# A kernel of attention and two matrix chains on one core: its first loads in three parts, its first scores in two steps, its last store in two halves, and some loads at other places in the plan

## Chip, core and metric

The kernel runs on one core of a Trainium2 chip. The metric is the device time of one execution in microseconds (us), the median of several runs. The engines are named as in the profile: PE is TensorE (PEld its weight loads), ACT is ScalarE, DVE is VectorE, POOL is GpSimd, SP is SyncE, which here only issues transfers (DMAs).

## The reference, cut to what matters

```python
# 4 batches, 8 heads, 512 local and 32 global positions, head size 64
s_g = scale * q_g @ k_all.T ;  out_g = softmax(s_g) @ v_all      # the 32 global queries see all keys
s_l = [scale * q_l @ k_g.T, banded(scale * q_l @ k_l.T, |i - j| <= 32)]
out_l = softmax(s_l) @ [v_g, v_l]                                 # local queries: global keys and a band
x = concat(out_g, out_l)  ->  (2176 tokens, 512)
h = x @ w_in                  # 512 -> 2048
g = h * clip(h + 3, 0, 6) / 6
y = g @ w_out                 # 2048 -> 512
z = max(y @ w1, y @ w2, y @ w3)   # 512 -> 768
out = z @ w_out2              # 768 -> 512
```

Inputs and output are float32; the weights come as 64-bit words that the kernel decodes (three vector steps and a copy for each block).

## The kernel before

The work has four stages that overlap at their borders. **Attention** goes over 4 batches times 4 pairs of heads (`pair`): load Q, K and V of the pair (tiles `qr`, `kr`, `vr`), scores into PSUM banks `s` or `bank` (L449), the row maximum with the band mask on DVE (L463), the exponential on ACT (L469), a sum and its reciprocal, the scaling on POOL (L494, tile `tbuf`), the transposes on PE (L506), their copies to `pt` (L410), and the product with V into `o` (L532). Each pair has two groups u = 0 and 1 of two query tiles v = 0 and 1 of 128 rows, so a group's scores are eight matmuls. After each two pairs the 32 global queries of both are done (`globals_`: L566, L592, L607). **First** (L673, three-pass products of split float32 operands) makes `x @ w_in` as soon as weights are decoded (`decode`, loads `raw<-in_w_in` at L642) and rows of x are there; it is put between the steps of the attention on PE. The gated result goes to DRAM (`gsA`, `gsB`, `gsC`). **Second** (L837) reads it back for `w_out`, **third** (L961, `quad`) makes the three products with w1, w2 and w3 and their maximum, written to DRAM as `hd`, and **fourth** (`single` L1116, `double` through `quad`) reads `hd` back (the loads of h, L1102 and L1128) and makes the output, which `send` stores (L1089).

No engine's order is written out by hand. Every step is an `op` with an engine, an assumed duration, a due time and the buffers that it reads and writes; `Plan.order` walks through time, and among the steps that could start on a free engine takes the one with the lowest due time. The sequence that results is the program; on each engine it runs in exactly this order. A changed duration, due time or split of one step can therefore change what stands where on every engine much later. `LAG` sets how early the loads of the third stage's weights may start.

At the very start PE writes ones into the score banks (`fill`, L395, four matmuls of 128 columns for each of six banks), and the first scores wait for all of them (`after=full`). The first pair's Q is loaded in two parts on SP's queue and its K in two parts on ACT's queue; part 0 holds what group u = 0 needs:

```python
for n, (t, src, cut, size) in enumerate(((Q, q_n, 256, NQ + SG), (K, k_n, 352, NK))):
    for i, (a, z) in enumerate(((0, cut), (cut, size)) if b + pr == 0 else ((0, size),)):
        e, issue = ("ACT", nc.scalar) if b + pr == 0 and n else ("SP", nc.sync)
```

The last `double` leaves two tiles of 128 tokens; the second is stored in two column halves of 128 x 256 (128 KB each), the last of them after the last copy out of PSUM on ACT (L412).

## Time and profile before

| | us |
|---|---|
| median of 3 runs | 733.19 |
| the 3 runs | 730.5, 733.19, 733.71 |
| the profiled execution, as timed | 731.45 |
| its span, first to last instruction | 729.2 |
| PE busy in it | 717.7 |
| DVE, ACT, POOL busy | 535.3, 411.0, 189.8 |
| PE's last matmul ends, from the span's start | 726.2 |

The time of an execution is its span and 2.25 us around it. Busy time is the time in which an engine had at least one instruction under way; since matmuls follow each other in a pipeline, a busy PE can still have been kept waiting for some hundred nanoseconds between two of them.

### The profile page before, as it was taken

How to read it: one execution, taken by the hardware profiler on the slowest of the kernel's cores; microseconds unless marked ns; L12 is line 12 of the kernel's file. 1: busy time of each engine (PE TensorE's matmuls, PEld its weight loads, DVE VectorE, ACT ScalarE, POOL GpSimd, SP SyncE). 2: the span in 40 equal slices, each digit the busy share in tenths (PEclk: the TensorE clock that was granted, in tenths of full speed). 3: DMA queues.
4: the chain of work that ended last, by engine and by line, in shares of the span. 5: the costliest groups of instructions: out<-in, count | busy, mean ns of one | idle time of the engine just before them, and what ended most of it. 6: DMA issues, size and time to landing. Idle time of an engine off the chain costs nothing.

```text
span 729.2 us, 14100 instructions
## 1 busy us (share of the span) xinstructions
PE 717.7 (98%) x5329; PEld 638.1 (88%) x5329; DVE 535.3 (73%) x1100; ACT 411.0 (56%) x858; POOL 189.8 (26%) x225
## 2 busy tenths in 40 slices
PE   8999999999999999999999999999999999999998
PEld 6777878788888899988898899898999999998998
DVE  6979676546777766589976768999877886485881
ACT  7997889555544444356663457673644334253552
POOL 6685869322203122111000001121210220011210
PEclk9999999999999999999999999999999999999999
DMA  7455775424368884676565669401453562355652
GB/s 279 129 180 193 253 256 192 153 72 165 140 209 295 317 307 171 233 260 195 174 206 156 202 196 312 127 2 32 133 172 134 173 228 69 102 170 198 175 159 88
DMA packets 73140, 131.34 MB, mean 180 GB/s; under 512 B 4976, under 2 KB 43632, under 8 KB 72048
## 3 DMA queue, kind: packets, MB, share of 16 engines
q1 hardware_dynamic: 72784, 130.13, 53.6%
q8 instruction: 42, 0.69, 0.4%
q10 hardware_dynamic: 288, 0.31, 0.1%
q14 instruction: 26, 0.21, 0.1%
HBM read 84.93 MB, written 45.48 MB: 179 GB/s over the span
## 4 chain that ended last, share of the span: by engine, by line
PE 79%; DMA 6%; DVE 5%; ACT 4%; POOL 3%; issue 2%; SPq 0%; ACTq 0%; DVEq 0%; POOLq 0%
PE bank L961 31%; PE bank L673 21%; PE bank L837 20%; PE s L506 2%; ACT tbuf L469 2%; POOL rq L655 2%; PE o L532 2%; PE s L449 1%; DMA raw<-in_w_in_dram 1%; DMA gsA<-rq 1%; DMA kr<-in_kn_dram 1%; PE bank L1116 1%; POOL tbuf L494 1%; DVE rr L655 1%; PE s L607 1%
## 5 line engine op out<-in xcount | busy, mean ns | idle before, releaser
L673 PE MATMUL bank<-rx,rw 128*128 128x512 f32 (+1 forms) x960 | 199.1, 363 | 1.1 <-DVE rq L685 1.1
L673 PEld LDWEIGHTS bank<-rx,rw 128*128 128x128 f32 x960 | 161.2, 188 | 26.8 <-issue 4.3
L837 PE MATMUL bank<-rr,rw 128*128 128x320 f32 (+2 forms) x912 | 155.1, 331 | 1.0 <-DVE rr L655 0.9
L837 PEld LDWEIGHTS bank<-rr,rw 128*128 128x128 f32 x912 | 140.2, 188 | 15.0 <-DVE rr L655 1.9
L961 PE MATMUL bank<-rw,rr 128*128 128x256 f32 (+2 forms) x648 | 99.7, 302 | 1.1 <-DVE rf L973 0.7
L961 PEld LDWEIGHTS bank<-rw,rr 128*128 128x128 f32 x648 | 90.6, 188 | 6.1 <-DVE rf L973 1.1
L760 ACT CAST rr<-fw 128x1024 fp32r<-128x1024 f32 (+2 forms) x76 | 62.1, 820 | 52.3 <-PE bank L837 40.5
L655 DVE TENSOR_TENSOR rr<-fw,rr 128x1024 fp32r<-128x1024 f32 (+2 forms) x76 | 71.7, 947 | 25.1 <-ACT rr L760 24.4
L655 POOL TENSOR_TENSOR rf<-rf 128x256 f32<-128x256 f32 (+2 forms) x35 | 37.5, 1080 | 157.2 <-DVE rf L655 58.8
L469 ACT ACTIVATE tbuf<-tbuf,nm 128x224 f32<-128x224 f32 x128 | 60.6, 479 | 11.0 <-DVE nm L463 10.9
L685 DVE SCALAR_TENSOR_TENSOR rq<-rq,bank 128x512 f32<-128x512 f32 (+1 forms) x60 | 37.1, 619 | 38.4 <-ACT rq L683 38.1
L494 POOL TENSOR_TENSOR tbuf<-tbuf,nm 128x448 f32<-128x448 f32 x64 | 61.0, 973 | 8.4 <-DVE nm L485 4.9
L683 ACT ACTIVATE rq<-bank,three 128x512 f32<-128x512 f32 (+1 forms) x60 | 37.9, 632 | 43.5 <-PE bank L673 40.3
L410 ACT COPY rf<-bank 128x512 f32<-128x512 f32 (+2 forms) x72 | 33.2, 468 | 39.9 <-PE bank L961 29.5
L961 PE MATMUL bank<-rw,re 128*128 128x256 f32 (+2 forms) x369 | 54.2, 292 | 0.7 <-DVE bank L410 0.7
L961 PE MATMUL bank<-re,rr 128*128 128x512 f32 x222 | 54.8, 391 | 0.0
L655 POOL TENSOR_TENSOR rq<-rq 128x256 f32<-128x256 f32 (+2 forms) x45 | 38.5, 861 | 54.1 <-DVE rq L655 49.5
L961 PEld LDWEIGHTS bank<-rw,re 128*128 128x128 f32 x369 | 49.4, 188 | 2.4 <-DVE bank L410 0.9
L961 PEld LDWEIGHTS bank<-re,rr 128*128 128x128 f32 x222 | 40.8, 188 | 8.1
L1055 DVE TENSOR_TENSOR rf<-rf,bank 128x320 f32<-128x320 f32 (+2 forms) x72 | 37.0, 528 | 13.0 <-PE bank L961 11.7
L463 DVE CUSTOM_DVE_ANT_0 tbuf<-s,mask 128x224 f32<-128x224 f32 x112 | 36.9, 383 | 6.7 <-PE s L449 6.4
L506 PE MATMUL s<-ident,tbuf 128*128 128x128 f32 x256 | 33.9, 276 | 0.4 <-POOL tbuf L494 0.2
(131 smaller groups left out, 1047.4 us busy)
## 6 DMA issues: line engine op xcount, KB each, us to landing
fw<-gsB SPq DMA_DIRECT2D x28, 512.0 KB, 4.8
raw<-in_w_dram SPq DMA_DIRECT2D x24, 512.0 KB, 4.3
fw<-gsC SPq DMA_DIRECT2D x28, 320.0 KB, 3.6
raw<-in_w_in_dram SPq DMA_DIRECT2D x16, 512.0 KB, 4.0
raw<-in_w_o_dram SPq DMA_DIRECT2D x16, 512.0 KB, 4.9
fw<-gsA SPq DMA_DIRECT2D x28, 256.0 KB, 2.8
gsB<-rq SPq DMA_DIRECT2D x6, 1024.0 KB, 5.1
rf<-hd SPq DMA_DIRECT2D x14, 384.0 KB, 4.9
```

The lines of the kernel that those rows point to most:

```text
L463: nc.vector.tensor_tensor_reduce(out=tb[hh]()[:, v, 0:WIN], in0=sb[hh]()[:, v * WIN:v * WIN + WIN], in1=mask[i // 2]()[:, i % 2], scale=-0 ...
L469: nc.scalar.activation(out=t, in_=t, func=ACTF.Exp, scale=-1.0, bias=nm()[:, 0, hh, v:v + 1], accum_out=nm()[:, 1, hh, v:v + 1])
L494: nc.gpsimd.tensor_tensor(out=t, in0=t, in1=r, op=ALU.mult)
L506: nc.tensor.transpose(FB[u][hh]()[:, at:at + 128], TB[u][hh]()[:, v, kb * 128:kb * 128 + 128], ident)
L655: ENG[e].tensor_tensor(out=out, in0=a, in1=b, op=f)
L673: nc.tensor.matmul(ps()[:, 0:m], lhsT=w[:, i, k], rhs=xs(c)[:, j, k], start=(k == 0 and s == 0), stop=(k == KC - 1 and s == 2))
L683: op("ACT", us, lambda ps=ps, m=m, out=out: nc.scalar.activation(out=out(), in_=ps()[:, 0:m], func=ACTF.Relu, bias=three), -100, r=[ps], w ...
L685: op("DVE", us, lambda ps=ps, m=m, out=out: nc.vector.scalar_tensor_tensor(out=out(), in0=out(), scalar=6.0, in1=ps()[:, 0:m], op0=ALU.min ...
L760: op("ACT", act(n) + 0.01, lambda: nc.scalar.copy(out=out(0), in_=src()), due, r=r, w=[(w, "hi")], what=what + "_hi")
L837: nc.tensor.matmul(A[e]()[:, 0:n], lhsT=w[:, 2 * fp + f, u, e], rhs=r[:, v, f], start=(seed is None and fp + f + s == 0), stop=(fp == 3 an ...
L961: nc.tensor.matmul(bank()[:, 0:n], lhsT=w[:, u, k], rhs=r[:, v, k], start=(start and k + s == 0), stop=(k == K - 1 and s == 2), skip_group ...
L1055: op("DVE", dve(n), lambda q=q, src=src, mv=mv: nc.vector.tensor_tensor(out=mv(q)(), in0=mv(q)(), in1=src(), op=ALU.max), -200, r=[bank], ...
```

## The change

It makes these edits. The first pair's Q is cut at columns 128 and 256 and its K at 224 and 352, so that part 0 is what query tile v = 0 needs (Q 128 x 128 and K 128 x 224), part 1 what v = 1 needs beyond it, and part 2 the rest. The first group's scores become two steps, one for each v, each with its own parts of Q and K as inputs, and what they write is named by v, so that the row maxima of v = 0 can follow the first step. `fill` writes 448 columns of each bank (three times 128 and once 64) and not 512. The last store goes out in two halves of 64 partitions, one issued by SP and one by ACT. The loads of h in `double` are due 18 and not 12 us before their product, and `LAG` is 94 and not 92.

```diff
-LAG = 92.0
+LAG = 94.0
...
     def fill(bank):
-        for j in range(4):
-            nc.tensor.matmul(bank[:, 128 * j:128 * j + 128], lhsT=ones, rhs=ones, start=True, stop=True)
+        for a in range(0, 2 * WIN, 128):
+            n = min(128, 2 * WIN - a)
+            nc.tensor.matmul(bank[:, a:a + n], lhsT=ones, rhs=ones[:, 0:n], start=True, stop=True)
...
-        for n, (t, src, cut, size) in enumerate(((Q, q_n, 256, NQ + SG), (K, k_n, 352, NK))):
-            for i, (a, z) in enumerate(((0, cut), (cut, size)) if b + pr == 0 else ((0, size),)):
+        for n, (t, src, cuts, size) in enumerate(((Q, q_n, (128, 256), NQ + SG), (K, k_n, (WIN, 352), NK))):
+            for i, (a, z) in enumerate(zip((0, *cuts), (*cuts, size)) if b + pr == 0 else ((0, size),)):
...
-                    out=t()[:, a:z], in_=src[b, pr][:, a:z]), s0 - 6 + i, w=[(t, i)] if b + pr == 0 else [t],
+                    out=t()[:, a:z], in_=src[b, pr][:, a:z]), s0 - 6 + i / 2, w=[(t, i)] if b + pr == 0 else [t],
...
-            need = [(Q, grp[0]), *((K, u) for u in range(grp[0] + 1))] if len(grp) == 1 else [Q, K]
-            head = op("PE", 0.62 * k, scores, s1, r=need, after=full if b + pr == 0 else (),
-               w=[x for u in grp for x in SB[u]] + [(t, "held") for u in grp for t in TB[u]], what="scores")
+            if b + pr + grp[0] == 0:
+
+                for v in range(2):
+                    head = op("PE", 0.31, lambda v=v, scores=scores: scores((v,)), s1 + v / 2, r=[(Q, v), *((K, x) for x in range(v + 1))],
+                              w=[(x, v) for x in SB[0]] + [(t, "held") for t in TB[0]], after=full, what="scores")
+            else:
+                need = [(Q, 2), (K, 1), (K, 2)] if b + pr == 0 else [Q, K]
+                head = op("PE", 0.62 * k, scores, s1, r=need,
+                          w=[x for u in grp for x in SB[u]] + [(t, "held") for u in grp for t in TB[u]], what="scores")
...
-    def send(o, t0, due, a=0, k=2):
-
-        def store():
+    def send(o, t0, due, a=0, k=2, parts=0):
+
+        def store(h=None):
             b, p = divmod(t0, SL)
             col = slice(256 * a, 256 * (a + k))
-            if b < B:
+            if h is not None:
+                (nc.scalar if h else nc.sync).dma_start(out=out[b * NQ + SG + p + 64 * h:b * NQ + SG + p + 64 * h + 64, col],
+                                                        in_=o()[64 * h:64 * h + 64, col])
+            elif b < B:
...
-        op("SP", 0.7, store, due, r=[(o, j) for j in range(a, a + k)], kb=128 * k, what="store")
+        r = [(o, j) for j in range(a, a + k)]
+        if parts:
+            for h in range(2):
+                op(("SP", "ACT")[h], 0.7, lambda h=h: store(h), due, r=r, kb=64 * k, what="store")
+        else:
+            op("SP", 0.7, store, due, r=r, kb=128 * k, what="store")
...
-               t - 12, r=rows(ts[i]), w=[(W, 1 - i)], kb=384, what="hload")
+               t - 18, r=rows(ts[i]), w=[(W, 1 - i)], kb=384, what="hload")
...
-            send(O[i], ts[i], t + 8 + i + (k - 1) / 4, a, k)
+            send(O[i], ts[i], t + 8 + i + (k - 1) / 4, a, k, last and i + a == 1)
```

Where it moves instructions: on PE the first difference is in the fills, the eight first scores stand in the same order with one wait more among them, and from the third pair on the attention's steps and `first` are interleaved otherwise. Counted over PE's whole order, its matmuls stand in 151 runs of one source line before and in 138 after; up to the end of the attention these are 139 and 128, and visits to `first` among them 42 and 35. No matmul is added or taken away: 28 fills, seven of them shortened, and 4,597 others. On DVE, ACT and POOL the order differs from the first batch on through the third stage; PE's last 868 matmuls and DVE's last 113 instructions, in the third and fourth stage, stand as before.

The first place is the start. On PE, the first scores before, with the semaphores that they wait for (`DMAHW0` to `DMAHW7` are those of the transfers, `kr` and `qr` the tiles of K and Q):

```order
L449 MATMUL s_162<-kr,qr 64x128 [waits DMAHW1_49,DMAHW0_49]
L449 MATMUL s_163<-kr,qr 64x128
L449 MATMUL s_162<-kr,qr 64x192
L449 MATMUL s_163<-kr,qr 64x192
L449 MATMUL s_162<-kr,qr 64x192
L449 MATMUL s_163<-kr,qr 64x192
L449 MATMUL s_162<-kr,qr 64x160
L449 MATMUL s_163<-kr,qr 64x160
```

And on PE at the same place after the change:

```order
L450 MATMUL s_162<-kr,qr 64x128 [waits DMAHW1_49,DMAHW0_49]
L450 MATMUL s_163<-kr,qr 64x128
L450 MATMUL s_162<-kr,qr 64x192
L450 MATMUL s_163<-kr,qr 64x192
L450 MATMUL s_162<-kr,qr 64x192 [waits DMAHW3_49,DMAHW2_49]
L450 MATMUL s_163<-kr,qr 64x192
L450 MATMUL s_162<-kr,qr 64x160
L450 MATMUL s_163<-kr,qr 64x160
```

The second four now wait for parts of their own, and the first four for smaller ones. On SP's queue at the start, before (V is `vr`, the second pair's loads are whole tiles of 576 and 608 columns):

```order
L426 DMA qr<-in_qn_dram 128x256
L426 DMA qr<-in_qn_dram 128x320
L426 DMA qr<-in_qn_dram 128x576
L426 DMA kr<-in_kn_dram 128x608
L429 DMA vr<-in_v_dram 128x640 x2
L426 DMA qr<-in_qn_dram 128x576 [waits DMAHW0_49]
L426 DMA kr<-in_kn_dram 128x608 [waits DMAHW1_49]
L642 DMA raw<-in_w_in_dram 128x4x256 [waits DMAHW2_49]
```

And after, where there is one transfer more ahead of the second pair's, and the loads of V wait for the first parts to land, because the eight semaphores are all taken:

```order
L427 DMA qr<-in_qn_dram 128x128 x2
L427 DMA qr<-in_qn_dram 128x320
L427 DMA qr<-in_qn_dram 128x576
L427 DMA kr<-in_kn_dram 128x608
L430 DMA vr<-in_v_dram 128x640 [waits DMAHW0_49]
L430 DMA vr<-in_v_dram 128x640 [waits DMAHW1_49]
L427 DMA qr<-in_qn_dram 128x576 [waits DMAHW2_49]
L427 DMA kr<-in_kn_dram 128x608 [waits DMAHW3_49]
```

The order on ACT's queue is K in three parts and not two, then its first exponentials. The second place is the attention's middle, on PE around the transposes of the third set of global queries (`tg`; `rx,rw` are operands of `first`), before:

```order
L673 MATMUL bank_135<-rx,rw 128x512 x3
L673 MATMUL bank_134<-rx,rw 128x512 x3
L506 MATMUL s_162<-ident,tbuf_142 128x128 x4
L506 MATMUL s_163<-ident,tbuf_144 128x128 x4
L673 MATMUL bank_134<-rx,rw 128x512 x3
L506 MATMUL s_164<-ident,tbuf_146 128x128 x4
L506 MATMUL s_165<-ident,tbuf_148 128x128 x4
L592 MATMUL s_166<-ident,tg 128x128 x4
L592 MATMUL s_162<-ident,tg 128x128
L673 MATMUL bank_134<-rx,rw 128x512 x3
L566 MATMUL s_163<-kr,qr 64x288 x2
L566 MATMUL s_164<-kr,qr 64x256 x2
```

And after:

```order
L680 MATMUL bank_134<-rx,rw 128x512 x3
L680 MATMUL bank_135<-rx,rw 128x512 x12
L680 MATMUL bank_134<-rx,rw 128x512 x3
L513 MATMUL s_163<-ident,tbuf_142 128x128 x4
L513 MATMUL s_164<-ident,tbuf_144 128x128 x4
L680 MATMUL bank_134<-rx,rw 128x512 x6
L513 MATMUL s_165<-ident,tbuf_146 128x128 x4
L513 MATMUL s_166<-ident,tbuf_148 128x128 x4
L599 MATMUL s_162<-ident,tg 128x128 x4
L599 MATMUL s_163<-ident,tg 128x128
L680 MATMUL bank_134<-rx,rw 128x512 x3
```

The same steps stand there with more of `first` between them at a visit. On SP's queue in the first batch, the loads of the weights of `first` (`raw`) among those of a pair, before:

```order
L699 DMA gsA<-rq 128x768
L642 DMA raw<-in_w_in_dram 128x4x256
L426 DMA qr<-in_qn_dram 128x576
L429 DMA vr<-in_v_dram 128x640
L426 DMA kr<-in_kn_dram 128x608
L429 DMA vr<-in_v_dram 128x640
L699 DMA gsA<-rq 128x1024
```

And after, where K is no longer behind a V, and the block of weights stands behind Q, K and V:

```order
L706 DMA gsA<-rq 128x768
L427 DMA qr<-in_qn_dram 128x576
L427 DMA kr<-in_kn_dram 128x608
L430 DMA vr<-in_v_dram 128x640
L649 DMA raw<-in_w_in_dram 128x4x256
L430 DMA vr<-in_v_dram 128x640
L706 DMA gsA<-rq 128x768
```

The third place is the end. On SP the rows from the first load of h on are the same as before but for the last, a store of 128x256 that becomes one of 64x256; the loads of h (L1128, now L1143) stand where they stood. On ACT the last rows before are these:

```order
L412 ACTIVATE rf<-bank_2649 128x256 [waits DMAHW3_49,DMAHW1_49,PE_49]
L412 ACTIVATE rf<-bank_2651 128x256 [waits DMAHW0_49,PE_49]
L1201 UNCONDITIONAL_BRANCH
```

And after, with the store's second half behind the last copy:

```order
L413 ACTIVATE rf<-bank_2624 128x256 [waits DMAHW5_49,DMAHW3_49,PE_49]
L413 ACTIVATE rf<-bank_2626 128x256 [waits DMAHW2_49,PE_49]
L1096 DMA out_dram<-rf 64x256 [waits Activation_49]
L1216 UNCONDITIONAL_BRANCH
```

## Rows read from the trace of the kernel before

**Rows 1.** The page: span, and each engine's busy time.
```profile
span 729.2 us, 14100 instructions
PE 717.7 (98%) x5329; PEld 638.1 (88%) x5329; DVE 535.3 (73%) x1100; ACT 411.0 (56%) x858; POOL 189.8 (26%) x225
```

**Rows 2.** Busy time by stretch: from:to, length, then each engine's.
```profile
0.00:3.90 3.90, 2.74 (x24) 2.48 (x24) 1.02 (x15) 1.28 (x1) 3.34 (x15) 1.00 0.51 149
3.90:28.10 24.20, 22.38 (x317) 16.61 (x319) 20.77 (x96) 21.67 (x81) 15.03 (x24) 1.00 0.67 236
28.10:205.00 176.90, 174.27 (x1778) 141.30 (x1773) 117.82 (x372) 132.71 (x370) 96.05 (x121) 1.00 0.51 177
205.00:600.00 395.00, 392.83 (x2357) 360.08 (x2356) 314.61 (x491) 199.07 (x317) 59.49 (x54) 1.00 0.58 191
600.00:726.20 126.20, 125.47 (x863) 117.67 (x862) 81.12 (x129) 55.90 (x91) 15.92 (x13) 1.00 0.44 141
```

**Rows 3.** The timeline at the start: start, length, engine and line.
```profile
0.73 0.90 ACTq L426 DMA_DIRECT2D kr<-in_kn_dram  x2
...
2.60 0.91 SPq L429 DMA_DIRECT2D vr<-in_v_dram  x2
2.73 1.06 PE L395 MATMUL bank<-ones 128*128 128x128 bf16 x8
...
5.52 0.39 DVE L463 CUSTOM_DVE_ANT_0 tbuf<-s,mask 128x224 f32<-128x224 f32 x1 [3.67 <-PE s L449]
```

**Rows 4.** Transfers issued in the first 12 us: count, size, time to landing.
```profile
kr<-in_kn_dram ACTq DMA_DIRECT2D x1, 176.0 KB, 3.1
qr<-in_qn_dram SPq DMA_DIRECT2D x1, 128.0 KB, 2.9
kr<-in_kn_dram ACTq DMA_DIRECT2D x1, 128.0 KB, 3.5
```

**Rows 5.** The chain that ended last, its pieces in the first 30 us.
```profile
3.91 1.50 PE s L449 x16
...
5.95 4.29 ACT tbuf L469 x18
...
22.58 0.29 DVE rx L549
...
27.56 1.83 PE o L532 x32
```

**Rows 6.** PE's timeline in the attention: visits to `first` and what follows.
```profile
31.10 0.97 PE L673 MATMUL bank<-rx,rw 128*128 128x512 f32 x3
32.00 1.00 PE L532 MATMUL o<-pt,vr 128*64 128x128 f32 x16
...
107.59 7.10 PE L673 MATMUL bank<-rx,rw 128*128 128x512 f32 x30
114.53 1.03 PE L506 MATMUL s<-ident,tbuf 128*128 128x128 f32 x8
115.32 0.95 PE L673 MATMUL bank<-rx,rw 128*128 128x512 f32 x3
116.11 1.03 PE L506 MATMUL s<-ident,tbuf 128*128 128x128 f32 x8
```

**Rows 7.** PE's waits between 28.1 and 726.2 us: total, times, longest.
```profile
PE bank L673 <- DVE rq L685: 1.1, 1, 1.1
PE s L449 <- DMA kr<-in_kn_dram: 1.1, 2, 0.6
```

**Rows 8.** The timeline at the end: the last copy, and SP's last stores.
```profile
718.12 8.85 SPq L1089 DMA_DIRECT2D out_dram<-rf  x5
...
726.22 0.38 ACT L412 ACTIVATE rf<-bank 128x256 f32<-128x256 f32 x1 [2.81 <-PE bank L961]
```

**Rows 9.** The stores issued from 724 us on, with time to landing.
```profile
out_dram<-rf SPq DMA_DIRECT2D x2, 128.0 KB, 1.7
out_dram<-rf SPq DMA_DIRECT2D x1, 256.0 KB, 2.0
```

More of the change, by code (lines that the diff above doesn't have):

```diff
@@ L393, in fill @@
     def fill(bank):
-        for j in range(4):
-            nc.tensor.matmul(bank[:, 128 * j:128 * j + 128], lhsT=ones, rhs=ones, start=True, stop=True)
+        for a in range(0, 2 * WIN, 128):
+            n = min(128, 2 * WIN - a)
+            nc.tensor.matmul(bank[:, a:a + n], lhsT=ones, rhs=ones[:, 0:n], start=True, stop=True)
     def filled(bank, after=()):
-        return op("PE", 0.43, lambda: fill(bank), -100, after=after, rel=0.4, what="fill")
+        return op("PE", 0.38, lambda: fill(bank), -100, after=after, rel=0.4, what="fill")
     full = [filled(bank) for bank in (*sbanks[:4], banks[6], banks[7])]
@@ L438, in pair, with scores @@
                 NM[u] = Buf(T["nm"])
-            def scores(grp=grp, SB=SB):
+            def scores(vs=(0, 1), grp=grp, SB=SB):
                 for u in grp:
-                    for v in range(2):
+                    for v in vs:
                         i = 2 * u + v
```

## The prediction

> **What bounds the kernel now.** I read the page's busy times first: PE is busy 717.7 of 729.2 us, and no other engine is near it [rows 1]. So the end comes where PE's own list of work ends, and the question for each edit is whether PE starts earlier, waits less or has less to do. The busy time by stretch says where PE is not busy [rows 2]. Up to 3.9 us it does only the fills. From 3.9 to 28.1 us, the first batch, it is idle 24.20 - 22.38 = 1.82 us while ACT is busy 21.67 us of 24.20. From 28.1 to 726.2 us it is idle in 698.1 us for 2.63 + 2.17 + 0.73 = 5.53 us, in waits of half a microsecond to one. After 726.2 us it has nothing left. All idle time between its first score and its last matmul is thus 7.35 us: what waiting alone can give back.
>
> The chain of waits tells which work sets the pace at the start: K's landing, the scores, then exponential after exponential on ACT from 5.95 us on, a DVE stretch from 22.58 us, and from 27.56 us PE [rows 5]. The reader is to see there that until about 27 us PE waits for the softmax, and from then on the softmax is fed into a PE that always has some of `first` to do.
>
> **The change part by part.**
>
> *First loads and scores.* The first scores begin at 3.91 us [rows 5], 0.08 after K's first part landed (issued 0.73, landing 3.1 later [rows 3, 4]). Of two parts issued at 0.73 the one of 176 KB took 3.1 and the one of 128 KB 2.9 us: 48 KB for 0.2 us. The new first part of K has 112 KB, 64 less, so it lands some 0.27 sooner, at 3.56, and Q's first part of 64 KB sooner than that. This is an estimate from two rows on two queues; its bounds are no gain at all and, if landing went by size alone, a part that is there before PE is free. Scores then begin at about 3.64.
>
> The fills must be over by then. The last eight begin at 2.73 and end 1.06 us later, one each 0.107 us if the last is as long as their 0.31 [rows 3], so the last starts at 3.48 and PE could issue a score at 3.58, shortened or not. Six shorter fills ahead of it give between 0 and 0.32 us, which nothing needs: I cost them at zero. If their cover goes, because K lands faster than I think, at most 0.3 us shows.
>
> The second gain is larger. The row maximum waits for all sixteen score records, 1.50 us [rows 5], and begins at 5.52 [rows 3]. Now it waits for half of them: 3.64 + 0.75 + 0.10 (as now from 5.42 to 5.52) = 4.49. That is 1.03 us earlier, and with it ACT's first exponential, at 5.95 now [rows 5]. The second step needs K's second part, which is issued one ACT issue later (0.90/2 = 0.45 us [rows 3]) and completes the 176 KB that landed at 3.83 before; I put it at 4.3, under the first step. The third parts go out 0.45 us later on both queues; the one of K took 3.5 us from 1.18 [rows 4], so 5.1 at the latest against scores that need it after the second step and a fill, not before 5.5. The loads of V now stand behind a wait for the first parts: from 2.60 us [rows 3] to about 3.6, ten microseconds ahead of the first product with V on PE, which is behind the transposes. Behind them in SP's queue the third pair's loads and the first weight block shift by tenths; I cost that at nothing while ACT has the sixteen exponentials of two pairs to do.
>
> What does PE get of the 1.03 us? About the 0.27 by which its own scores move, at least. At most all, if it loses 0.76 of its 1.82 us idle. I take 0.8, near the upper end, since ACT is the busy engine of the stretch and PE's idle time there is what ACT leaves. Bounds: 0.2 to 1.0.
>
> *The new order in the attention.* PE's list has 11 runs of one kind of matmul fewer up to the end of the attention. What a run costs is seen at `first`: thirty matmuls in one visit take 114.53 - 107.59 = 6.94 us, 0.231 each, while three alone hold PE for 32.00 - 31.10 = 0.90 us, not 0.69 [rows 6]. Thirteen such short visits between 31 and 116 us, of which this is the longest and the last, 116.11 - 115.32, the shortest, hold it 0.79 to 0.90 us: 0.10 to 0.21 more than three in a long run, 0.15 in the middle. Eleven runs fewer are 11 x 0.15 = 1.65 us. Lower bound nothing, if these changes of kind hid waits that now show as idle; upper bound 11 x 0.21 = 2.3. I take 1.65, because from 28.1 us on only 2.63 us of 176.9 are idle, so PE was working, not waiting, at most of these places.
>
> *The waits after 28.1 us.* A new order keeps none of them in its place. Two are for K (1.1 us) and one for the gated result (1.1 us) [rows 7]. I leave the sum of 5.53 us as it is: zero, with bounds of 2.5 us less (the two lines of rows 7 gone and a little more) and 3 us more (three times the longest).
>
> *Loads of h, and `LAG`.* On SP every load of h stands where it stood, so that edit moves nothing: zero. `LAG` shifts weight loads of the third stage among the loads of the second; PE's idle time there is inside the 2.17 us of 205 to 600 us, and so inside the bounds above.
>
> *The last store.* PE ends at 726.20, ACT's copy 0.38 later [rows 8]. The last 128 KB take 1.7 us to land, 256 KB took 2.0 [rows 9]: 0.15 for 64 KB less. SP's issue is over 0.37 us after that copy; ACT's takes 0.45. So between 0.15 less and 0.1 more; I take 0. The Trainium skill says in "DMA: Bandwidth & Descriptors", section "Issuing engines are not separate DMA queues", that transfers started by different engines run on the same 16 DMA engines and that starting them on several saves only the issue time; by it the halves land together when the whole would have, and this term is 0 as well, where the two rows of landing by size alone would make it 0.15.
>
> **The sum.** -0.8 - 1.65 + 0 + 0 + 0 = -2.45 us, 729.0 for the profiled execution's 731.45. That execution lies 1.74 us below the median shown, and the three runs spread over 3.2 us. I carry the change to the middle of the two, 732.3, and forecast **729.8**. Half a per cent, 3.7 us, is about what a measurement of this kernel can tell from no change, so this is the same by that measure.
>
> **The rivals.**
>
> *Only the start counts, or not even that.* PE is 98% busy, so what ACT gains is spent in a PE that has the same matmuls to do; and if a short visit costs little more than its matmuls once its neighbours are counted, the eleven runs give nothing. For it: no matmul goes. Against it: the 0.90 against 0.69 us. It gives -1.2 to +1, 731.1 to 733.3.
>
> *More than the sum.* The order also removes the waits. For it: one K load that stood behind a V load no longer does, and both waits for K are of that kind; the new order does less of `first` before the attention ends, so the softmax is less often the one that waits. With 2.5 us of waits gone the change is -2.45 - 2.5 = -4.95 (727.3), at the upper bounds of both main terms -1.0 - 2.3 - 2.5 = -5.8 (726.5).
>
> *Slower: a weight block comes late.* At one place in the first batch the load of a block of `w_in` now stands behind Q, K and V of a pair. PE's list is fixed, so the matmul of `first` that needs the block stops everything behind it, scores and transposes too, and with them ACT and DVE. No wait for such a block stands among PE's waits [rows 7], but how near they are is not shown. Those three loads have 288 + 304 + 320 KB; at the 236 GB/s of that early stretch [rows 2] they take 3.9 us. It decides against the change from the point where such waits add up to 2.45 us; two full delays give -2.45 + 7.8 = +5.3, 737.6.
>
> *The change does not do what it says.* That holds for the loads of h, which move in the plan's numbers and nowhere in the program. It is in the sum.
>
> **How the numbers follow.** The forecast, -1.2 to -3.6 us: 0.45. Only the start or less, -1.2 to +1: 0.20. More than the sum, beyond -3.7: 0.25. Late weights, beyond +1: 0.10, of which 0.07 beyond +3.7. The range leaves out the far parts of the two outer cases, about 0.08 below 726.8 and 0.1 above 733.3. The likeliest case's own range is 728.7 to 731.1. Faster by over 0.5% is the third case and the edge of the first, 0.27; slower 0.07; the rest 0.66.
>
> **What would show it.** In the profile after: the first scores at 3.5 to 3.8 us, the first row maximum at 4.3 to 4.7, the first exponential near 4.9; PE's idle time between 3.9 and 28 us at about 1.2; the attention ended some 2 us earlier by the last product with V; the same spacing of the fourth stage; the last landing after the last copy unchanged within 0.15. Wrong would be: a first row maximum still above 5.2 (the second parts late); PE idle after 28 us above 8 (the order brought waits); waits of L680 for a weight block; fewer runs but the attention no shorter (the price of a run was read wrongly).

## The result: slower, 738.7 us

The changed kernel takes 738.71 us (median of 5 runs, 737.62 to 742.01), the kernel before beside it 732.24 (730.50 to 733.71): a ratio of 1.0095, interval 1.0073 to 1.0117. The forecast was 729.8, its range ended at 733.3. The profiled execution of after took 741.79 us and is one of the two longest of the five.

The page after, to set against [rows 1]: PE works 2.1 us more in a span 10.6 us longer.

```profile
span 739.8 us, 14078 instructions
PE 719.8 (97%) x5329; PEld 642.5 (87%) x5329; DVE 535.8 (72%) x1100; ACT 409.1 (55%) x853; POOL 193.7 (26%) x230
```

Busy time by stretch, cut like [rows 2] (columns: stretch, length, busy time of PE, PEld, DVE, ACT and POOL, granted clock, DMA share, GB/s). In the second PE is idle 2.82 us instead of 1.82, in the third 8.80 instead of 2.63. The granted clock, 1.00 in all of them before, is 0.98 in the third and 0.99 in the last.

```profile
3.90:28.10 24.20, 21.38 (x318) 16.41 (x313) 20.57 (x86) 19.79 (x70) 13.92 (x23) 1.00 0.60 209
28.10:205.00 176.90, 168.10 (x1733) 137.53 (x1730) 114.51 (x376) 132.06 (x374) 97.15 (x123) 0.98 0.52 176
205.00:600.00 395.00, 393.99 (x2369) 360.94 (x2366) 312.75 (x491) 197.01 (x312) 58.93 (x53) 1.00 0.58 190
600.00:735.90 135.90, 133.27 (x896) 124.85 (x894) 86.93 (x137) 58.60 (x97) 20.34 (x18) 0.99 0.45 142
```

PE's waits over the whole span (total, times, longest) are up to three times those of [rows 7], and mostly of other kinds: the global normalization `tg`, K again, a bank copy of the last stage. None is for a block of the weights of `first`.

```profile
PE s L599 <- DVE tg L590: 3.7, 2, 3.3
PE s L450 <- DMA kr<-in_kn_dram: 3.6, 4, 2.3
PE bank L968 <- DVE bank L411: 2.6, 1, 2.6
PE o L539 <- DVE pt L411: 1.8, 2, 1.4
PE s L599 <- ACT pt L411: 1.2, 1, 1.2
```

The timeline of after shows what a long wait leaves behind it. The 32 scores behind the wait of 2.27 us take 2.15 us, the same 32 at 109.87 us take 1.37. Three matmuls of `first` behind the wait of 3.28 us take 1.63 us; [rows 6] has three in 0.95.

```profile
83.16 2.15 PE L450 MATMUL s<-kr,qr 64*64 64x128 f32 x32 [2.27 <-DMA kr<-in_kn_dram]
...
109.87 1.37 PE L450 MATMUL s<-kr,qr 64*64 64x128 f32 x32
114.52 1.40 PE L599 MATMUL s<-ident,tg 128*128 128x128 f32 x5 [3.28 <-DVE tg L590]
115.58 1.63 PE L680 MATMUL bank<-rx,rw 128*128 128x512 f32 x3
```

In stretches of 2 us the granted clock there (third column from the right) is 0.50 to 0.75, so part of the time at 1.2 GHz instead of 2.4, and 1.00 before the waits. In the profiled execution of before it is 1.00 throughout.

```profile
84.00:86.00 2.00, 2.00 (x22) 1.57 (x15) 0.77 (x5) 0.23 (x1) 1.26 (x1) 0.50 0.79 222
86.00:88.00 2.00, 2.00 (x9) 1.59 (x8) 0.36 (x1) 1.08 (x2) 0.00 (x0) 0.75 0.94 316
...
114.00:116.00 2.00, 1.48 (x6) 1.27 (x7) 2.00 (x13) 1.59 (x5) 1.84 (x2) 0.58 0.58 170
116.00:118.00 2.00, 2.00 (x24) 1.25 (x24) 1.71 (x10) 2.00 (x8) 1.98 (x4) 0.57 0.94 354
```

Where the delay arises is read from the last matmul of `first` (the matmuls of one line: shortest, median, longest in ns, first and last start in us). In before it starts at 305.6 us:

```profile
L673 PE MATMUL bank<-rx,rw x960: 305/389/504, 31.1 to 305.6; 128*128 128x512 f32 x116, 128*128 128x320 f32 x76
```

and in after at 313.3, 7.7 later; the last product with V is only 2.3 us later, at 204.0, but 24 matmuls of `first` fewer stand ahead of it:

```profile
L680 PE MATMUL bank<-rx,rw x960: 305/389/794, 29.2 to 313.3; 128*128 128x512 f32 x116, 128*128 128x320 f32 x76
```

So the loss lies in the attention. By the first single tile of the last stage the delay is 6.7 us (665.8 for 659.1). This execution loses 3.3 more behind it, with the bank copy's 2.6 and a granted clock of 0.50 after that, too; the three shorter ones of the five lie 3.1 to 4.2 us below it.

### The profile page after: what moved, and what is told of

Read it like the earlier page. It is cut to its first block, busy times and chain, and to the rows that moved or that the text cites. A ratio compares the mean times of both kernels' runs of the same rounds, so it can differ in the third digit from the quotient of the medians.

```text
span 739.8 us, 14078 instructions
## 1 busy us (share of the span) xinstructions
PE 719.8 (97%) x5329; PEld 642.5 (87%) x5329; DVE 535.8 (72%) x1100; ACT 409.1 (55%) x853; POOL 193.7 (26%) x230
## 4 chain that ended last, share of the span: by engine, by line
PE 81%; ACT 7%; DMA 6%; DVE 3%; POOL 1%; issue 1%; SPq 0%; ACTq 0%; DVEq 0%
PE bank L968 32%; PE bank L680 22%; PE bank L844 20%; ACT tbuf L476 3%; DMA kr<-in_kn_dram 2%; PE s L513 2%; DMA raw<-in_w_in_dram 2%; PE o L539 1%; PE s L450 1%; PE bank L1131 1%; ACT pt L411 1%; DVE rq L634 1%; PE s L614 1%; DMA fw<-gsA 1%; DVE rr L662 1%
## 5 line engine op out<-in xcount | busy, mean ns | idle before, releaser
L680 PEld LDWEIGHTS bank<-rx,rw 128*128 128x128 f32 x960 | 163.0, 189 | 24.7 <-issue 2.6
L662 POOL TENSOR_TENSOR rq<-rq 128x256 f32<-128x256 f32 (+2 forms) x47 | 42.8, 914 | 58.7 <-DVE rq L662 37.1
L411 ACT COPY rf<-bank 128x512 f32<-128x512 f32 (+2 forms) x69 | 31.4, 463 | 43.5 <-PE bank L968 34.4
L662 DVE TENSOR_TENSOR rf<-rf 128x384 f32<-128x384 f32 (+4 forms) x50 | 27.8, 589 | 7.2 <-DMA rf<-hd 7.0
```

The source lines that it names most:

```text
L411: (nc.scalar.copy if eng == "ACT" else nc.vector.tensor_copy)(out=out, in_=in_)
L662: ENG[e].tensor_tensor(out=out, in0=a, in1=b, op=f)
L680: nc.tensor.matmul(ps()[:, 0:m], lhsT=w[:, i, k], rhs=xs(c)[:, j, k], start=(k == 0 and s == 0), stop=(k == KC - 1 and s == 2))
```

## The experiments

All kernels below were timed in 5 rounds with the kernel before on the same chip. To part the edits from the order, the planner is replaced by a list, read off one of the two kernels or put together from both, so that edits and order can be combined freely:

```diff
-        for o in plan.order():
+        for o in replay(plan):        # the steps in a written-out order, with engines and buffers placed as listed
```

| kernel | us | ratio to before, interval | PE idle 4 to 205 us | last `first` starts |
|---|---|---|---|---|
| before | 732.2 to 732.8 | 1 | 4.4 | 305.6 |
| after | 738.7 | 1.0095 (1.0073 to 1.0117) | 11.6 | 313.3 |
| edits_old_order | 734.36 | 1.0026 (1.0011 to 1.0042) | 5.0 | 305.5 |
| old_edits_new_order | 738.38 | 1.0075 (1.0058 to 1.0092) | 9.8 | 314.2 |
| fills_alone | 738.16 | 1.0077 (1.0062 to 1.0092) | 5.5 | 308.2 |
| split_alone | 732.68 | 1.0003 (0.9985 to 1.0021) | 5.6 | 305.9 |
| lag_alone | 732.90 | 0.9999 (0.9982 to 1.0015) | 4.4 | 305.0 |
| split_old_order | 732.98 | 1.0006 (0.9993 to 1.0019) | 4.2 | 305.4 |
| fills_store_old_order | 733.10 | 1.0011 (0.9996 to 1.0027) | 3.2 | 305.5 |
| early_row_maxima | 734.85 | 1.0026 (1.0007 to 1.0044) | 4.3 | 306.5 |
| two_waits_mended | 739.43 | 1.0090 (1.0072 to 1.0108) | 10.3 | 313.6 |
| one_wait_covered | 739.58 | 1.0090 (1.0066 to 1.0113) | 8.7 | 314.1 |
| waits_kept_warm | 735.43 | 1.0040 (1.0026 to 1.0053) | 7.4 | 311.2 |
| weights_early_new_order | 754.02 | 1.0284 (1.0258 to 1.0310) | 17.6 | 325.7 |
| weights_late_old_order | 749.42 | 1.0227 (1.0199 to 1.0255) | 17.6 | 322.8 |
| new_order_to_28 | 737.52 | 1.0063 (1.0042 to 1.0083) | 6.3 | 309.3 |
| new_order_to_60 | 738.90 | 1.0069 (1.0045 to 1.0092) | 9.9 | 311.3 |
| old_order_to_60 | 737.63 | 1.0056 (1.0034 to 1.0077) | 7.6 | 311.6 |
| h_loads_moved | 731.89 | 0.9990 (0.9976 to 1.0003) | 3.9 | 304.9 |
| split_and_h_loads_moved | 733.51 | 1.0013 (0.9999 to 1.0028) | 4.2 | 305.1 |

The last two columns come from one profiled execution of each kernel, the times from all of them. PE's idle time leaves out what PE does without use: in waits_kept_warm the 40 useless matmuls count as busy.

### The edits or the order

**edits_old_order** is the changed kernel, with the order of before written out in place of the planner's.

> All five edits of the change, but every instruction stands where it stood in the order of the kernel before; the new halves of a split step stand side by side. Theory 1 (the re-made order lost the time, the edits themselves give about what the start showed, 0.5 us): 0 to 1 us under the kernel before, 731.2 to 732.2 us, PE idle about 11, no granted clock under 1.00. Theory 2 (the edits themselves lost it: more transfers and more semaphores at the start delay what follows): 5 to 8 us above the kernel before, 737 to 740 us, PE idle near 20.

**old_edits_new_order** is the kernel before with the changed kernel's order.

> The instructions of the kernel before, in the order of the changed kernel; no load, score, fill or store is split. Theory 1: 5 to 8 us above the kernel before, 737 to 740 us, with the waits of PE for the K load near 83 us (2.3), for the global normalization near 114 us (3.3) and a granted clock under 1.00 behind them. Theory 2: within 1 us of the kernel before, 731 to 733 us.

The first ends its first stage at 305.5 us, the second at 314.2. The order carries the whole loss of that stage without one edit, and the edits lose nothing there without the order. Theory 1 holds in this, and misses by the sign of a small number: the edits bring nothing, they cost 0.26%. One expectation for old_edits_new_order was missed: PE waits 3.61 us for `tg` near 113 us, with a clock of 0.50 from 114 to 122, but not for K at 83 us, and the kernel is as slow without that wait. The timeline of PE at the start of edits_old_order shows why the first scores' 0.5 us (3.91 before) do not arrive: the scores of the second group, u = 1, wait for K's third part.

```profile
3.40 1.45 PE L450 MATMUL s<-kr,qr 64*64 64x128 f32 x16
4.79 0.55 PE L396 MATMUL s<-ones 128*128 128x128 bf16 x4
6.37 0.81 PE L450 MATMUL bank<-kr,qr 64*64 64x160 f32 x16 [1.03 <-DMA kr<-in_kn_dram]
```

Two edits alone, each with the planner free to order, and later `LAG` alone:

```diff
 fills_alone:   -        for j in range(4):                       (512 columns)
                +        for a in range(0, 2 * WIN, 128):         (448 columns; 0.38 for 0.43 in the plan)
 split_alone:   the loads' cuts (128, 256) and (WIN, 352), and scores((v,)) for v in range(2)
 lag_alone:     -LAG = 92.0
                +LAG = 94.0
```

> Only the shorter fills (448 columns of each bank instead of 512, 0.38 instead of 0.43 us in the plan); the planner orders freely and moves some 130 rows of PE. Theory 1: not decided by the edit but by the order that comes of it; as the kernel before has the order with few waits, 2 to 8 us above it, 734 to 740 us, all of it in waits of PE behind 28 us. Theory 2: within 1 us of the kernel before, since no load and no semaphore is added.

> Only the loads in three parts and the first scores a tile at a time; the planner orders freely and moves some 80 rows of PE. Theory 1: as with the fills alone, 2 to 8 us above the kernel before, in waits that lie elsewhere than those of the changed kernel. Theory 2: the whole loss, 5 to 8 us above the kernel before, with the waits at the start (first 28 us) above 7 us.

> The kernel before with the lead of the later weights' loads 94 instead of 92 us; the planner orders freely, 12 rows of PE and some 55 of DVE move, all behind the first 300 us. Theory 1 and W (the loss is in the order of the first 200 us, which stays): 731 to 734 us. Rival (the lead costs by itself, as weights of the later stages come later): 734 us or more, with the waits of PE behind 300 us above the 3 us of before.

The edit that only shortens seven matmuls, six of them ahead of the first load's landing, costs 0.77%, with a clock of 1.00 in its profile and less than half of the loss in the first stage (2.6 of the 5.7 us by which its span is longer); the one that adds loads and signals costs nothing, against both theories' figures for it. `LAG` moves PE's rows only in the second stage and later, and costs nothing. So what the shorter fills cost here is what their number does to the order (in the old order, below, they and the halved store are not told from before), and a re-made order is not always a bad one.

### The edits apart, in the old order

**split_old_order** has the split loads and scores alone, **fills_store_old_order** the fills and the halved store.

> Only the loads in three parts and the first scores a tile at a time, all in the order of the kernel before. If the 1.9 us that the five edits cost in the old order come from the split loads (the third parts of Q and K land 1.2 us later): 733.5 to 735.5 us, first scores 0.2 us earlier, second scores 0.3 to 0.5 us later. If not: 731.5 to 733 us.

> Only the shorter fills and the last store in two halves by SP and ACT, in the order of the kernel before. If the 1.9 us come from the split loads: 731.5 to 733 us. If they come from the last store or the fills: 733.5 to 735.5 us, and the last copy to the end of the span takes more than the 2.6 us of before.

Neither is told from before. The store is read from the traces: from the last copy's end to the span's end before takes 2.60 us [rows 1, 8]; fills_store_old_order has 725.96 + 0.38 to 729.6, 3.26. Over all profiled executions it is 2.59 to 2.95 us with the whole store and 3.22 to 3.31 with the halves, so the halves cost about half a microsecond. The two halves of that run (issue in ns, then time to landing: shortest, median, longest):

```profile
L1090 SPq DMA_DIRECT2D out_dram<-rf x1: 554/554/554, 726.4 to 726.4; - x1
L1090 ACTq DMA_DIRECT2D out_dram<-rf x1: 568/568/568, 726.4 to 726.4; - x1
...
DMA to landing us min/median/max: 2.0/2.2/2.3
```

The other 1.3 us or so of edits_old_order's 1.9 are not in the first stage. Its profile has 1.2 us more of PE's idle time than before's between 205 and 690 us, 0.8 of it behind 670. There, single executions in this same order differ by more: 0.03 us of idle time in fills_store_old_order, 0.72 in before, 2.48 in split_old_order. So I have not pinned these 1.3 us down.

**early_row_maxima** asks why the first row maximum came at 5.01 and not 4.49. In the program it waits for one signal, which PE raises with the last score that writes the bank, the seventh of eight, so with the second tile's. Here the two maxima stand ahead of the second tile's scores:

```diff
 order:  ... 13 scores v=0, 14 scores v=1, ..., 16 rowmax, 18 rowmax ...
      -> ... 13 scores v=0, 16 rowmax, 18 rowmax, 14 scores v=1, ...
```

> All five edits in the order of the kernel before, and the two row maxima of the first tile stand ahead of the second tile's scores, so that they need no longer wait for both; in return the second tile's scores wait until the maxima have read the bank. First row maximum at 4.2 to 4.5 us instead of 5.0, first exponential at 4.7 to 4.9 instead of 5.44, the second tile's scores 0.5 to 1 us later. Theory 1 (what the start gains is taken up by the next load that PE waits for): total within 1 us of the five edits in the old order, 733.5 to 735.5 us. Rival (the start is the path and 0.6 us of it come through): 732.5 to 734 us.

The timeline of DVE, and of PE:

```profile
4.47 0.39 DVE L470 CUSTOM_DVE_ANT_0 tbuf<-s,mask 128x224 f32<-128x224 f32 x1 [2.62 <-POOL ident masks.py:197]
...
3.40 0.92 PE L450 MATMUL s<-kr,qr 64*64 64x128 f32 x8
4.93 1.21 PE L450 MATMUL s<-kr,qr 64*64 64x192 f32 x8 [0.61 <-DVE nm L470]
```

The maximum comes at 4.47 as the prediction had it, the first exponential at 4.91; in return PE waits 0.61 us for DVE to have read the bank, and the first stage ends 1.0 us later than in edits_old_order. Softmax half a microsecond earlier than in edits_old_order (where the first exponential starts at 5.44) brings PE nothing. That a step of PE later costs is seen in this one execution, not in the medians, 734.85 and 734.36.

### What in the order

Where the two long waits of after come from, its trace shows. The load of K that PE waited for at 83 us was issued at 75.2, behind two weight blocks, and landed 7.8 us later; the load at the same place in before, issued at 74.1, also behind two blocks, took 5.4; why it took longer in after is not shown. And the global normalization `tg`, which PE waited for at 114 us, stands on DVE behind four decoding steps (timeline of after):

```profile
111.06 1.77 DVE L634 SCALAR_TENSOR_TENSOR rq<-rq,raw 128x512 int32<-128x512 int32 x2
112.75 1.28 DVE L637 SCALAR_TENSOR_TENSOR rq<-raw,rq 128x512 int32<-128x512 int32 x2
113.95 0.51 DVE L590 TENSOR_SCALAR tg<-tg,g 128x576 f32<-128x576 f32 x1
```

**two_waits_mended** takes the changed kernel's order and moves two groups (steps of the plan by number):

```diff
 DVE: the global normalization 667 ahead of the decoding 277, 284, 278, 285 (and of one gating step)
 PE:  four steps of first (12 matmuls) ahead of the scores 624, 640 that waited for K
```

> The changed kernel with two of its rows moved: on DVE the global normalization (the one that PE waited for 3.28 us at 114.5) stands four rows of weight decoding earlier, on PE twelve matmuls of the first stage stand ahead of the scores that waited 2.27 us for K at 83.2. Theory 1 (PE's in-order work stands behind late things, and a wait of that length also lowers the granted clock behind it): the two waits go, 5.5 us, and with them the stretches of granted clock 0.83 at 80 to 90 and 110 to 120 us, some 2 us more: 731 to 734 us. Rival (the waits only show that DVE and the transfers are behind, so other waits take their place): within 2 us of the changed kernel, 737 to 740 us.

In this kernel the row maxima of the two moved score steps stand ahead of them in the list and so read what the banks held before. The wait for K is gone, that for `tg` became one for a bank which DVE's row maxima free behind the same decoding: 3.42 us for 3.28. **one_wait_covered** has only PE's half, with the twelve matmuls moved ahead and the maxima behind their scores.

> The changed kernel; only twelve matmuls of the first stage (one visit) stand ahead of the scores that waited 2.27 us for K at 83.2 us, instead of behind them. Theory W: the wait at 83 us and the clock of 0.83 behind it go, but the matmuls that cover it are missing later, as PE has no other first-stage work until the next weight block is decoded: within 1.5 us of the changed kernel, 737 to 740 us. Rival (each wait is a loss of its own): 2.3 us and some 1.5 us of clock less, 734 to 736 us.

The wait of 2.27 us at 83 us is gone, the total is not better; the rival's 734 to 736 falls. Up to 112.70 PE waits 3.35 us for `tg`, as in after, and now the clock stays at 0.50 for longer, as the stretches of 2 us show (after had 1.00 again from 118):

```profile
114.00:116.00 2.00, 2.00 (x18) 1.25 (x17) 1.74 (x10) 2.00 (x8) 1.98 (x4) 0.50 1.03 387
...
120.00:122.00 2.00, 2.00 (x11) 2.00 (x10) 0.10 (x2) 1.80 (x4) 0.24 (x2) 0.50 0.78 172
122.00:124.00 2.00, 2.00 (x15) 1.82 (x14) 1.06 (x2) 1.50 (x4) 0.00 (x0) 0.87 0.97 346
```

**waits_kept_warm** leaves the order alone and fills the two waits with useless matmuls, which was meant to change only the clock:

```diff
+    def warm(buf, n):
+        for j in range(n):
+            nc.tensor.matmul(buf()[:, 0:128], lhsT=ones, rhs=ones, start=True, stop=True)
...
+                if (b, pr, grp[0]) == (2, 0, 0):
+                    warm(SB[0][0], 14)
...
+                if (b, pr, cs[0]) == (1, 3, 0):
+                    warm(fb, 26)
```

> The changed kernel in its own order; in its two longest waits PE does useless matmuls of ones (14 ahead of the scores that waited 2.27 us for K, 26 ahead of the transposes that waited 3.28 us for the global normalization), written to a bank that the step behind them overwrites. If the lowered clock costs time by itself: the granted clock stays at 1.00 from 80 to 120 us where it was 0.83 twice, and some 2 to 3.4 us come back, 735 to 737 us, first stage over by 310 to 311.5. If the clock behind the waits costs nothing, as PE would only wait again: 738 to 740 us, first stage over at 313.

PE's timeline at the two places, and the stretch behind the first:

```profile
81.38 0.94 PE L400 MATMUL s<-ones 128*128 128x128 bf16 x14 [0.18 <-ACT xg L626]
82.55 1.37 PE L456 MATMUL s<-kr,qr 64*64 64x128 f32 x32 [0.23 <-DMA kr<-in_kn_dram]
...
109.65 2.14 PE L456 MATMUL s<-kr,qr 64*64 64x128 f32 x32 [2.07 <-DMA kr<-in_kn_dram]
111.72 2.46 PE L400 MATMUL s<-ones 128*128 128x128 bf16 x26
114.02 0.71 PE L607 MATMUL s<-ident,tg 128*128 128x128 f32 x5
...
84.00:86.00 2.00, 2.00 (x9) 1.65 (x10) 0.86 (x4) 2.00 (x6) 0.99 (x1) 1.00 0.71 232
```

735.43 us: 3.3 us, half of the loss, comes back for 40 matmuls that compute nothing; by the ratios, 1.0040 for 1.0095, it is 4.0. An estimate of the clock's part comes from all runs of both: the mean granted clock is 0.994 over the five of after and 0.998 over the eleven here, which is 4.3 and 1.7 us of the span, so some 2.6 us of what came back is clock. Behind the first wait the 32 scores take 1.37 us, not 2.15. At 110 us the clock still fell, behind a wait of 2.07 us for K that I had not filled.

**Weights.** In after the last load of `w_in` is issued at 113.5 us, in before at 99.1. Two kernels exchange only the 112 steps that load and decode `w_in` between the orders.

> The changed kernel; only the 112 steps that load and decode the sixteen half blocks of w_in (SP loads, ACT, DVE and POOL decoding) stand at the places that they have in the order of the kernel before; PE's order is as in the changed kernel but for one group. Theory W (the new order serves the attention first on DVE and ACT, so the weight blocks come later, the last load at 113.5 instead of 99.1 us, and PE runs out of first-stage matmuls to put between late attention steps): most of the loss comes back, 731 to 735 us, last weight load near 100 us, first stage over by 306 to 309 us. Rival (the attention steps of PE themselves stand in a worse order): 736 to 740 us, first stage over at 312 to 315 us.

> The kernel before; only the 112 steps that load and decode w_in stand at the places that they have in the order of the changed kernel. Theory W: 736 to 741 us, last weight load after 110 us, PE waits in the first stage for blocks or behind them, first stage over by 311 to 315 us. Rival (PE's attention order): within 2 us of the kernel before, 731 to 734 us.

Both are far worse than either parent, and theory W falls as stated: early weights do not mend the new order. PE waits there for K (4.5 us in two waits), for weight blocks (3.8), for `tg` (3.0) and for an exponential (2.3). But both lists are mixtures that no plan made, so they price the mixing too, and not the weights' place alone. Its other half is shown: late weights stop PE at `first`, as the prediction's rival had it (timeline of weights_late_old_order):

```profile
136.61 0.98 PE L673 MATMUL bank<-rx,rw 128*128 128x512 f32 x2 [4.63 <-ACT rw L646]
```

**Where in time.** Three kernels with all edits follow one order for all steps that its plan starts by 28 or 60 us, and then the other:

```diff
 new_order_to_28, new_order_to_60: new order up to there, old behind
 old_order_to_60:                  old order up to there, new behind
```

> The five edits; the first 28 us in the new order, all behind in the old order. If the loss is laid down at the start: 736 to 741 us. If behind it: 731 to 735 us, first stage over by 305 to 308.

> The five edits; the steps that the changed kernel's plan starts in its first 60 us in the new order, all others behind them in the old order. If the loss is laid down in the first 60 us (weight blocks and attention already apart by then): 736 to 741 us, first stage over by 311 to 315. If it comes from the order behind 60 us (the waits of 2.27 and 3.28 us at 83 and 114): within 2 us of the kernel before, 731 to 735 us, first stage over by 305 to 308.

> The five edits; the first 60 us in the old order, all behind in the new order. If the loss is laid down in the first 60 us: 731 to 735 us. If it comes from the order behind: 736 to 741 us, with waits of more than 2 us of PE between 80 and 120 us.

All three lose 0.56 to 0.69%, of which 0.26% is the edits' by edits_old_order, so both answers were wrong: no one stretch of the new order carries the loss. Either part of it is enough, or the seam is: these runs cannot tell the two apart. new_order_to_60 gets a wait for K that neither parent has (its timeline):

```profile
70.14 2.17 PE L450 MATMUL s<-kr,qr 64*64 64x128 f32 x32 [4.18 <-DMA kr<-in_kn_dram]
```

### The loads of h

In the changed kernel they move nowhere. **h_loads_moved** is the kernel before with two of them really ahead of four small stores on SP; **split_and_h_loads_moved** does the same to split_alone.

```diff
 SP:  ... 2602 store (4 transfers), 2647 hload, 2648 hload ...
   -> ... 2647 hload, 2648 hload, 2602 store (4 transfers) ...
```

> The kernel before; two loads of h of the last stage (the pair that SP issued at 771.8 us less 100, that is at 671.8 us) really moved ahead, past the four small stores that SP issues from 669.5 to 671.3 us; nothing else moves. If those stores hold the loads back: the wait of PE near 676 us (0.72 us in the profiled run of before, 2 to 2.6 us with a granted clock under 1.00 behind it in others) goes, the median falls by 0.5 to 2 us, 730.5 to 732 us. If the loads wait for their buffer or for the transfers and not for the stores: no difference, within 0.5 us of the kernel before.

> The loads and first scores split, planner's own order of split_alone, and the same two loads of h moved ahead of the four small stores. split_alone ran level with the kernel before. If the stores hold the loads back: 729.5 to 732 us, below both. If not: 731.5 to 733 us.

No difference in either. SP's timeline of h_loads_moved shows the reason: with the stores out of the way the three loads take SP 5.33 us, as it waits between them, and PE's wait near 677 us is still 0.99. So the stores do not hold them back. No kernel of the study beats the kernel before by more than can be measured.

```profile
668.73 5.33 SPq L1128 DMA_DIRECT2D rf<-hd  x3
674.10 2.04 SPq L1092 DMA_DIRECT2D out_dram<-rf  x4
```

## Why the prediction was wrong

**What bounds.** Right in the main: the time went with PE's idle time and clock. They are not all of it: in fills_alone and new_order_to_28, whose profiles have a clock of 1.00 to the last matmul, idle time makes 3.8 and 3.9 us of the 5.7 and 6.5 by which their spans are longer; the rest is in the busy time of the same matmuls, 719.6 and 720.3 us for 717.7.

**First loads and scores, -0.8: came to nothing.** The scores began at 3.41, better than 3.64. Two steps failed. "Now it waits for half of them": it did not, the signal comes once for the bank, and the maximum began at 5.01. "The one of K took 3.5 us ..., so 5.1 at the latest": K's third part was issued at 1.7 and took 4.1 us, so it landed at 5.8, and the second group's scores waited 0.56 us for it. Even where the maximum did come at 4.47, PE had nothing of it; "I take 0.8, near the upper end, since ACT is the busy engine" is refuted: PE's idle time in the first batch rose by 1.0 us (2.82 for 1.82). The timeline of after:

```profile
3.41 1.45 PE L450 MATMUL s<-kr,qr 64*64 64x128 f32 x16
...
5.01 0.39 DVE L470 CUSTOM_DVE_ANT_0 tbuf<-s,mask 128x224 f32<-128x224 f32 x1 [3.16 <-PE s L450]
...
5.84 0.81 PE L450 MATMUL bank<-kr,qr 64*64 64x160 f32 x16 [0.56 <-DMA kr<-in_kn_dram]
```

Transfers of after issued in the first 3 us (count, size, time to landing), to set against [rows 4]: small first parts land 0.7 us sooner, and the parts behind them, unchanged in size, later.

```profile
qr<-in_qn_dram SPq DMA_DIRECT2D x1, 160.0 KB, 4.0
qr<-in_qn_dram SPq DMA_DIRECT2D x2, 64.0 KB, 2.2
kr<-in_kn_dram ACTq DMA_DIRECT2D x1, 128.0 KB, 4.1
kr<-in_kn_dram ACTq DMA_DIRECT2D x1, 112.0 KB, 2.4
```

**New order, -1.65: not seen.** In after 7.2 us more idle time between 4 and 205 us and, by the clock of 0.83 in each of the stretches 80 to 90 and 110 to 120 us, up to 3.4 us of slow clock make 10.6 for a delay of 7.7. That leaves room for the saving, but the same sum scatters over the other orders, from 1.8 us too little (new_order_to_28) to 4 too much; so it is not shown. The price itself does not hold up. It was read at visits to `first`, and of the 11 runs fewer only 7 are such visits (42 to 35). In the traces, new_order_to_28 has 138 runs up to the last product with V where before has 139, and 2.6 us more busy time at the same clock; split_alone has 130, and only 0.5 us less (717.2).

**Waits after 28.1 us, 0 with at most +3: the step that failed.** "I leave the sum of 5.53 us as it is": idle time in the attention alone rose by 6.2 us, and all of it after 28.1 us is 12.4 (8.80 + 1.01 + 2.63) for 5.53, beyond the 8 that the prediction itself had named as a sign of being wrong. Besides, a long wait has a second price, which the bound left out: the clock behind it. By waits_kept_warm that is some 3 us of the loss. The forecast weighed only what the new order removes. Of the other orders of the attention that were tried, split_alone's ran level, the others lost 0.6% to 2.8%; I should have put the centre of this term above zero and its upper end near 10.

**Loads of h and `LAG`, 0: right.** Both were tried alone, the loads by really moving them, which the change does not do.

**Last store, 0: too low by about half a microsecond.** After ends 3.25 us behind its last copy (736.17 + 0.38 to 739.8), before 2.60. The sentence cited from the Trainium skill's "DMA: Bandwidth & Descriptors", section "Issuing engines are not separate DMA queues", led to 0 as well, and the measurement differs: the halves took 0.56 us to issue for 0.33, and 2.0 and 2.3 us to land for the whole's 1.7.

**The slower rival, 0.10.** Its 737.6 is near the result by luck, for its mechanism did not occur: no matmul of after waited for a weight block. The blocks do come later in the new order, but exchanging them did not bring the time back, so the lateness goes with the loss and is not shown to be its cause. What makes one order of the attention better than another as a whole stays open; taking single waits away moved them on.

## What to carry to other kernels

When an edit feeds numbers to a planner, cost the re-made order first and the edit second: run the edit in the old order and the old program in the new one, and the two prices fall apart in two runs. In a kernel that is 98% busy on one engine a new order has little idle time to win and much to lose (here none of those tried won), so its waits get a range that reaches up. And a long wait of PE, here of some 2 us and more, is to be priced with the slow matmuls behind it.

## What the runs showed of the hardware

A wait of 2.07 to 4.63 us in the middle of a busy PE was followed by a granted clock of 0.50 (1.2 GHz) while PE worked again, in every kernel that had one, but not every time: behind 2.08 us at 56 and 2.26 us at 87 us in weights_early_new_order the clock stayed at 1.00, and behind 2.42 us at 121 us until PE waited again. Shorter waits were followed by it too: in new_order_to_60 one of 1.05 us at 448 us, with 1.5 us idle in all from 446 to 450 (0.50 from 450 to 452), and in three kernels one of 1.05 to 1.13 us at 6 us (0.50 from 8 to 10), while edits_old_order had 1.03 us there and kept 1.00. How long it stayed low differed for nearly the same wait: until about 118 us behind 3.28 us in after, until about 122 behind 3.35 us in one_wait_covered, and all the way from 110 to 120 us (mean 0.50) behind 3.07 us in old_order_to_60. Halving a store over two engines did not halve anything: each half of 64 rows was longer to issue (0.55 to 0.57 us for 0.33) and later to land (2.0 and 2.3 us for 1.7) than the whole.

The Trainium skill, "TensorE: Matmul & The Clock Gate", section "Part 1: The HAM clock gate", says that the clock is set by how busy PE has been recently; the filled wait at 82 us agrees with it, with a clock of 1.00 behind it where after had 0.50 (84 to 86 us).
